# First pass of a fused attention and SwiGLU kernel: transposes and weight joins moved behind the masks, raw weights in six places

## The chip, the cores and the metric

The kernel runs on one core of one Trainium2 chip. The metric is device microseconds of one execution, the median of several runs. The engines are named as in the profile: PE (TensorE, with its weight loads PEld), DVE (VectorE), ACT (ScalarE), POOL (GpSimd), and SP, which here issues nearly all DMAs.

## The reference

```python
# q, k, v: (8, 8, 576, 64) float32; tau = 0.02
scores = q @ k.T / sqrt(64)
thresh = max(scores, axis=-1) - tau
scores = where(scores >= thresh, scores, -1e9)
attn = exp(scores - max(scores)) ; attn /= sum(attn) + 1e-9
x = (attn @ v) -> (B, H, S, D) to (B*S, H*D) = (4608, 512)
g = x @ w_gate                 # (512, 1536)
h = g * sigmoid(g) * (x @ w_val)
out = h @ w_out                # (1536, 512)
```

## The kernel before

The work is 32 pairs of heads (8 batches with 4 pairs each), and each pair has 576 queries and keys. A tile of attention is up to 128 queries of one pair. For one tile, PE computes the scores of both heads into PSUM (`scores`, L505), DVE takes the row maxima (L497), ACT makes a threshold (L528) and the exponentials (L529), and DVE masks them by the threshold and sums them (L532, then L534 and L535 for the reciprocal). After that PE transposes the masked scores (`flip_steps`, L576 or L578, L582 to L588), ACT copies the transposes to SBUF (L585, L592), and PE multiplies them with v (`attend_tile`, L609 and L611); ACT copies that result out (L614). The PSUM that holds a tile's scores is used again by the next tile, so the scores of the next tile wait for the masks of this one, head by head.

The first batch is done in two passes, in program order and in a schedule written out by hand. The first pass takes pairs 0 to 3 with two tiles of 128 queries each (n from 0 to 3, x from 0 to 1). The second takes the other three tiles of the same pairs (n from 4 to 7, in the order of pairs 3, 0, 1, 2), and between them PE does the first part of the feed-forward block (`fill`, L625). In one turn of the loop over tiles, program order is: scores and maxima of this tile; the point `maxima`; product with v of an earlier tile; exponentials of this tile; transposes of the tile before; the point `flipped`; masks of this tile; the point `masked`; scaled unit matrices (first pass, L548) or fill; the point `end`. At each point the table `STEPS` names side work that is put into the engines' queues there. Every engine works through its queue in order, so a step's place decides what it stands in front of. After the two passes the remaining batches run in an order that a planner (`Plan`) writes out.

The steps are these:

- `weights`, `weights 2`: `fetch_weights` issues on SP the two DMAs of one weight piece (or of two pieces) as raw 64-bit words (L344). A piece needs a free raw place, and a place comes free when its piece has been joined.
- `split`: ACT makes the upper part of a piece (L360). In the first pass POOL makes the lower part (L362) and clamps the upper one (L353). In the second pass ACT makes the lower part too (L364), and POOL clamps at `clamp_split`. The lower parts use three buffers by turns.
- `shift`: one DVE operation on the upper part (L383).
- `join`: one DVE operation that puts the sign back (L390) and, on POOL, the sum of both parts (L400), by `add_lower`.
- `qk`, `rest`: DMAs of a pair's k and first 256 columns of q, or of the rest of q (L436). `v`: DMAs of a pair's v (L479, L480).
- `scale`: POOL scales a q tile (L440), in the order pair 2, pair 3, rests of pairs 3, 0, 1, 2, pair 4.
- `prepare`: DVE transposes k and q of the next pair (L738, L742). `turn`, `turn last`: DVE transposes the rest of q of a pair (L797).

`STARTS` lists what SP issues ahead of the first tile, after the q and k of pairs 0 and 1.

Of the kernel before, what the change touches and what calls it, by code (L numbers as in the profile page):

```python
# [27 lines left out]
class Plan:  # L28
# [94 lines left out]

STARTS = ("weights", "v", "weights", "qk", "weights", "v", "v", "weights")

STEPS = {
    (0, 0, "flipped"): ("qk",),
    (0, 1, "maxima"): ("prepare",),  # L130
    (0, 1, "masked"): ("split",),
    (0, 1, "end"): ("scale",),
    (1, 0, "flipped"): ("split", "shift"),
    (1, 0, "masked"): ("join",),
    (1, 1, "flipped"): ("weights 2", "prepare"),
    (1, 1, "masked"): ("split", "shift"),
    (1, 1, "end"): ("join",),
    (2, 0, "maxima"): ("rest", "weights 2"),
    (2, 0, "flipped"): ("rest",),
    (2, 0, "masked"): ("shift", "scale", "split", "join"),  # L140
    (2, 0, "end"): ("weights 2",),
    (2, 1, "maxima"): ("scale", "prepare", "v", "rest"),
    (2, 1, "flipped"): ("rest", "split"),
    (3, 0, "flipped"): ("shift",),
    (3, 0, "end"): ("join",),
    (3, 1, "maxima"): ("shift", "split", "turn last"),
    (3, 1, "flipped"): ("weights 2", "scale", "prepare"),
    (3, 1, "masked"): ("split",),
    (3, 1, "end"): ("turn", "shift", "scale"),
    (4, 0, "flipped"): ("turn", "qk"),  # L150
    (4, 1, "maxima"): ("scale",),
    (4, 1, "masked"): ("scale",),
    (4, 2, "end"): ("turn",),
# [4 lines left out]
def kernel(  # L158
# [152 lines left out]
    wpieces = deque()  # L311
# [5 lines left out]
    for f in range(0, DFF, FW):  # L317
        for c in range(NCC):
            wpieces.append((wgv[:, :, c, f:f + FW], [w[c * P:(c + 1) * P, f:f + FW] for w in (w_gate, w_val)],
                            len(wpieces) % 4))  # L320
    nf = TW // DM2
    wplaces = deque([6, 4, 5, 3, 4, 5, 4, 5])
    for e in range(2):
# [5 lines left out]
    fetched, split, used = deque(), deque(), set()  # L329
    joined = []  # L330

    def fetch_weights(n=1):
        for _ in range(n):
            if not wpieces or wpieces[0][2] in used:
                return
            dst, srcs, place = wpieces.popleft()
            used.add(place)
            m = 2 if len(srcs) == 2 else nf
            to = places[place].bitcast(U64).rearrange("p (m n) -> p m n", m=m)
            if len(srcs) == 1:  # L340
                nc.sync.dma_start(out=to, in_=srcs[0])
            else:
                for x, src in enumerate(srcs):
                    nc.sync.dma_start(out=to[:, x, :], in_=src)  # L344
            fetched.append((dst, place))
# [30 lines left out]
    def shift_weights(n=1):  # L376

        steps = [split.popleft() for _ in range(min(n, len(split)))]
        if any(up is x for up, place, lo in steps for x in unclamped):
            clamp_split()  # L380
        for up, place, lo in steps:
            ub = up.bitcast(U32)
            nc.vector.tensor_scalar(out=ub, in0=ub, scalar1=3, scalar2=None, op0=ALU.logical_shift_left)  # L383
        shifted.extend(steps)

    def join_weights(n=None):
        steps = shifted[:n]
        for up, place, lo in steps:
            ub = up.bitcast(U32)
            nc.vector.scalar_tensor_tensor(out=ub, in0=words(place, up, 1), scalar=0x80000000, in1=ub,  # L390
                                           op0=ALU.bitwise_and, op1=ALU.bitwise_xor)
            used.discard(place)
        unsummed.extend(steps)
        del shifted[:n]
        add_lower(min(1, len(unsummed)))
# [311 lines left out]
    rest = list(range(TA, NT + 1))  # L707
# [19 lines left out]
    def prepare(seg):  # L727
        i = seg["i"]
        if i in kept:
            seg.update(kept[i])  # L730
            return
        assert i > NP or (i, 0) in scaled
        qr, kr = raws[i][0:2]
        if i < NP:
            kept[i] = None
            qT = qkp.tile([P, S], F32, name="qT")
            kT, rest_ = kTs[i], rests[i]
            nc.vector.transpose(out=kT, in_=kr)  # L738
            if i == 0:
                nc.vector.tensor_scalar(out=scl, in0=tau_s, scalar1=0.0, scalar2=SCALE, op0=ALU.is_ge, op1=ALU.mult)  # L740
                nc.vector.tensor_scalar(out=qr[:, 0:QA], in0=qr[:, 0:QA], scalar1=scl, scalar2=None, op0=ALU.mult)
            nc.vector.transpose(out=qT[:, 0:QA], in_=qr[:, 0:QA])  # L742
            if i == 0:
                nc.vector.tensor_scalar(out=cap, in0=tau_s, scalar1=0.0, scalar2=2e38, op0=ALU.is_ge, op1=ALU.mult)
                nc.vector.tensor_scalar(out=cap, in0=cap, scalar1=-1e38, scalar2=None, op0=ALU.add)
                nc.vector.scalar_tensor_tensor(out=cut, in0=tau_s, scalar=-1.0, in1=cap, op0=ALU.mult, op1=ALU.min)
            later.append((rest_, i))
            kept[i] = {"kT": kT, "qT": rest_, "q0": QA}
        else:
            qT, kT = qr, kr  # L750
            nc.vector.transpose(out=kT, in_=kT)
            nc.vector.transpose(out=qT, in_=qT)
        seg.update(kT=kT, qT=qT, q0=0)
# [25 lines left out]
    def start(what):  # L779
        if what == "weights":  # L780
            fetch_weights()
        elif what == "v":
            load_v(unloaded.popleft())
        elif what == "qk":
            fetch_qk(unfetched.popleft())
        else:
            rest_load()

    for what in STARTS:
        start(what)  # L790
    last = iter(())

    def turn():
        to, i = later.popleft()
        assert (i, 1) in scaled
        turned_rests.add(i)
        nc.vector.transpose(out=to, in_=raws[i][2])  # L797

    def steps(n, x, point):
        for what in STEPS.get((n, x, point), ()):  # L800
            if what in ("rest", "v", "qk"):
                start(what)
            elif what == "turn last":
                later.rotate(1)
                turn()
            elif what == "prepare":
                prepare(segs[n + 1])
            elif what == "weights 2":
                fetch_weights(2)
            else:  # L810
                {"scale": scale_next, "turn": turn, "split": split_weights, "shift": shift_weights,
                 "join": join_weights}[what]()

    begun = deque([scores(segs[0], 0, first_pss)])
    for n, seg in enumerate(segs[:2 * NP]):
# [3 lines left out]
        for x, t in enumerate(seg["tiles"]):  # L819
# [4 lines left out]
            if (n, x) == (0, 0):  # L824
                second_pss = [ps_s.tile([P, 2, 512], F32, name="sc") for _ in range(2)]
                begun.append(scores(seg, seg["tiles"][1], second_pss, later=True))
                next(begun[0])
            next(go)
            steps(n, x, "maxima")
            if n >= NP:  # L830
                join_weights(1)
# [51 lines left out]
            last = go  # L883
# [1673 lines left out]
    rest = [b for b in banks if b.fixed is None and b not in mine]  # L2557
# [213 lines left out]
```

## Time and profile before

| | |
|---|---|
| runs | 1331.33 us median of 3 (1331.12 to 1332.28) |
| the profiled execution | 1332.23 us, of which the span from first to last instruction is 1330.4 |
| granted TensorE clock | 1.000 |
| busy, share of the span | PE 99%, PEld 84%, DVE 82%, ACT 67%, POOL 71% |
| first pass, scores of (1,0) to scores of (4,0) | 15.24 to 46.29 us |
| second pass, up to the first scores of the planned part | 46.29 to 123.47 us |
| DMA | 209.81 MB, mean 158 GB/s |

Times of lines are in microseconds from the start of the span. The timeline merges instructions that follow each other on one engine and line; in brackets stands the idle time before, and what ended it. Busy times of PE are modelled ends. Nearly all of the span is the planned part, which starts where the second pass ends.

### The profile page before, as it was taken

The page shows a single profiled execution, that of the slowest core. Times are in us where ns is not written, and L with a number is a line of the kernel's source. Part 1 is how long each engine was busy: PE and PEld are TensorE (multiplying, and loading weights), DVE is VectorE, ACT ScalarE, POOL GpSimd, SP SyncE. Part 2 cuts the span into 40 slices and gives each one's busy share as a digit, 9 for nine tenths or more (in the row PEclk, how much of TensorE's full clock was granted, in tenths as well). Part 3 has the DMA queues.
Part 4 walks back from the last instruction along what each step waited for, and adds up shares of the span by engine and source line. Part 5 has one row for each costly group of instructions (what it writes and reads, how often), then busy time and mean ns, then how long its engine had stood idle before and what let it go on. Part 6 is the DMA issues. An engine that isn't in the chain of part 4 may idle for free.

```text
span 1330.4 us, 41756 instructions
## 1 busy us (share of the span) xinstructions
PE 1320.2 (99%) x16294; PEld 1119.1 (84%) x16294; DVE 1092.4 (82%) x2900; ACT 892.9 (67%) x2336; POOL 951.1 (71%) x1137
## 2 busy tenths in 40 slices
PE   8999999999999999999999999999999999999998
PEld 7777777777788878888888888887888889999998
DVE  7799988878887788878888887888788888767986
ACT  6898877677755777787777777777777775444300
POOL 3788597565695979756995779677975798866720
PEclk9999999999999999999999999999999999999999
DMA  8853334456647544656265746655465627465341
GB/s 178 220 180 108 71 81 120 126 155 178 161 168 228 168 152 114 202 157 222 71 203 165 235 107 193 180 166 154 111 202 157 217 74 227 152 208 189 96 171 40
DMA packets 230884, 209.81 MB, mean 158 GB/s; under 512 B 167968, under 2 KB 185376, under 8 KB 223008
## 3 DMA queue, kind: packets, MB, share of 16 engines
q1 hardware_dynamic: 226768, 206.22, 52.4%
q8 instruction: 129, 2.11, 0.7%
q10 hardware_dynamic: 3920, 0.92, 0.3%
q14 instruction: 67, 0.55, 0.1%
HBM read 169.08 MB, written 38.01 MB: 156 GB/s over the span
## 4 chain that ended last, share of the span: by engine, by line
PE 94%; ACT 3%; DMA 1%; POOL 1%; DVE 1%; SPq 1%; issue 0%; ACTq 0%; DVEq 0%
PE pb L1190 14%; PE px L1820 12%; PE sc L2111 10%; PE pa L1190 10%; PE xa L2211 10%; PE pe L1190 6%; PE po L1498 6%; PE sc L2601 5%; PE py L1820 4%; PE pe L1385 3%; PE pb L2601 2%; PE pg L1423 2%; PE pa L2601 2%; PE pv L1423 2%; PE py L1829 2%; PE sc L1820 1%
## 5 line engine op out<-in xcount | busy, mean ns | idle before, releaser
L2159 DVE SCALAR_TENSOR_TENSOR pall<-sc,th,pall 128x288 f32<-128x288 f32 x504 | 244.2, 514 | 39.3 <-ACT pall L2157 20.2
L2157 ACT ACTIVATE pall<-sc,nm 128x288 f32<-128x288 f32 x504 | 232.7, 497 | 34.9 <-DVE pall L2159 34.7
L1190 PE MATMUL pb<-xall,big 128*128 128x256 f32 x864 | 205.9, 381 | 0.0
L2189 DVE STREAM_TRANSPOSE pall<-pall 128x576 f32<-128x576 f32 x252 | 188.4, 764 | 19.2 <-ACT pall L2187 9.4
L971 POOL TENSOR_TENSOR big<-big 128x128 f32<-128x128 f32 (+3 forms) x226 | 167.1, 748 | 43.5 <-ACT big L1325 21.7
L2187 ACT ACTIVATE pall<-pall,ri 128x288 f32<-128x288 f32 x380 | 175.8, 527 | 27.3 <-DVE ri L2175 26.3
L1190 PEld LDWEIGHTS pb<-xall,big 128*128 128x128 f32 x864 | 161.0, 190 | 24.1 <-issue 2.2
L971 POOL TENSOR_TENSOR hall<-hall,tmp 128x512 f32<-128x512 f32 x80 | 102.1, 1278 | 87.9 <-DVE hall L1249 66.9
L2132 DVE TENSOR_REDUCE mx<-sc 128x2 f32<-128x576 f32 x168 | 125.5, 747 | 45.2 <-PE sc L2111 45.1
L2111 PE MATMUL sc<-kT,qT 64*32 64x288 f32 (+1 forms) x5376 | 144.5, 345 | 0.0
L1190 PE MATMUL pa<-xall,big 128*128 128x256 f32 x576 | 137.6, 382 | 0.0
L2111 PEld LDWEIGHTS sc<-kT,qT 64*32 64x32 f32 x5376 | 95.3, 106 | 48.3 <-issue 8.3
L2211 PE MATMUL xa<-pall,vall 64*32 64x288 f32 x4032 | 128.7, 404 | 0.0
L1190 PEld LDWEIGHTS pa<-xall,big 128*128 128x128 f32 x576 | 107.9, 190 | 17.3 <-issue 2.2
L2211 PEld LDWEIGHTS xa<-pall,vall 64*32 64x32 f32 x4032 | 74.0, 107 | 46.9 <-issue 4.0
L2184 POOL TENSOR_SCALAR pall<-pall,ri 128x288 f32<-128x288 f32 x124 | 63.5, 523 | 49.0 <-DVE ri L2175 46.9
L2168 ACT COPY sums<-sums 32x6 f32<-32x6 f32 x336 | 66.6, 198 | 31.3 <-DVE pall L2159 26.2
L1190 PE MATMUL pe<-xall,big 128*128 128x256 f32 x352 | 83.9, 381 | 0.0
L2134 DVE TENSOR_REDUCE mx<-sc 128x1 f32<-128x288 f32 x168 | 75.0, 447 | 0.0
L1190 PEld LDWEIGHTS pe<-xall,big 128*128 128x128 f32 x352 | 66.3, 190 | 10.3 <-ACT xlast L2223 0.7
L971 POOL TENSOR_TENSOR hall<-hall 128x384 f32<-128x384 f32 (+2 forms) x69 | 70.3, 1032 | 0.8
L971 POOL TENSOR_TENSOR big<-hall 128x384 f32<-128x384 f32 (+2 forms) x69 | 65.6, 972 | 4.3 <-PE pa L1190 4.2
(402 smaller groups left out, 3055.7 us busy)
## 6 DMA issues: line engine op xcount, KB each, us to landing
big<-sums_hbm SPq DMA_DIRECT2D x30, 1280.0 KB, 7.6
big<-sums_hbm SPq DMA_DIRECT2D x30, 1024.0 KB, 7.4
vall<-in_v_dram SPq DMA_DIRECT2D x112, 144.0 KB, 4.0
big<-sums_hbm SPq DMA_DIRECT2D x54, 256.0 KB, 3.6
sums_hbm<-big SPq DMA_DIRECT2D x36, 256.0 KB, 3.6
out_dram<-big SPq DMA_DIRECT2D x32, 256.0 KB, 3.1
qT<-in_q_dram SPq DMA_DIRECT2D x112, 72.0 KB, 4.2
kT<-in_k_dram SPq DMA_DIRECT2D x112, 72.0 KB, 3.0
```

The source lines that it names most:

```text
L971: nc.gpsimd.tensor_tensor(out=out, in0=a, in1=b, op=op)
L1190: nc.tensor.matmul(ps[:, i], w[:, k_, i * P:(i + 1) * P], x[:, k_, :], start=first and i == k_ == 0, stop=True, skip_group_check=True)
L1498: nc.tensor.matmul(ps, h(f), w[:, f, :], start=(f == 0), stop=(f == NF2 - 1))
L1820: nc.tensor.matmul(ps, a[:, f, :], ws[n][:, f, :], start=bank_ not in begun, stop=True, skip_group_check=True)
L2111: nc.tensor.matmul(pss[h][(slice(g * G, (g + 1) * G), *part)], qT[hs, col:col + G], kT[hs, c * SH + keys[0]:c * SH + keys[1]], start=True, ...
L2132: rs.append(job("DVE", 0.72, lambda n=n, tile_=tile_: nc.vector.tensor_reduce(out=mx[:, n:n + 2, 0], in_=tile_[:, :, 0:SH], axis=AX.X, op= ...
L2157: ej = job("ACT", 0.42, lambda x=x, n=n: nc.scalar.activation(ps[x], scs[x], AF.Exp, bias=nm[:, n:n + 1]), ej, masks.get((h, u - 1)), rank=0)
L2159: masks[x] = job("DVE", 0.45, lambda x=x, n=n: nc.vector.scalar_tensor_tensor(out=ps[x], in0=scs[x], scalar=th[:, n:n + 1], in1=ps[x], op0 ...
L2187: scaled.append(job("ACT", 0.46, lambda x=x, n=n: nc.scalar.activation(x, x, AF.Copy, scale=ri[:, n:n + 1]), rj, rank=rank))
L2189: seg["turned"].append(job("DVE", 0.72, lambda both=both: nc.vector.transpose(out=both, in_=both), *scaled, rank=rank))
L2211: nc.tensor.matmul(holds[a].ap()[x * G:(x + 1) * G, 0:SH].rearrange("d (i q) -> d i q", q=G), vr[rs, h, j, ds], p[rs, h, :, j, :], start=( ...
L2601: nc.tensor.matmul(both.ap(b_)[:, at_ * P:(at_ + 1) * P], ws[x], xd[x], start=b_ not in begun, stop=True, skip_group_check=True)
```

## The change

The table of steps of the first pass is written anew. `prepare` moves from the points in front of the masks to the point behind them, and joins move from the end of a tile to behind the masks of another one, so that a tile has either a `prepare` or a join there. The shift of (1,0) goes, and later shifts stand in the tile of their join. q and k of pair 3 are issued on SP among the `STARTS`, and not at (0,0). The first six raw weight pieces have a place each (the new ones lie in `xall` and `extra`), and later pieces go through the first four. The split at (2,0) goes; at the end of (4,0), in the second pass, a join, a fetch, a shift, a split and a clamp are added. `steps` knows `clamp` as a further step. The order of PE's instructions is the same in both kernels.

```diff
--- before.py
+++ after.py
@@ -123,31 +123,32 @@
 
 
 
-STARTS = ("weights", "v", "weights", "qk", "weights", "v", "v", "weights")
+STARTS = ("weights", "v", "weights", "qk", "weights", "v", "qk", "v", "weights")
 
 STEPS = {
-    (0, 0, "flipped"): ("qk",),
     (0, 1, "maxima"): ("prepare",),
     (0, 1, "masked"): ("split",),
     (0, 1, "end"): ("scale",),
-    (1, 0, "flipped"): ("split", "shift"),
-    (1, 0, "masked"): ("join",),
-    (1, 1, "flipped"): ("weights 2", "prepare"),
-    (1, 1, "masked"): ("split", "shift"),
-    (1, 1, "end"): ("join",),
-    (2, 0, "maxima"): ("rest", "weights 2"),
+    (1, 0, "flipped"): ("split",),
+    (1, 0, "masked"): ("prepare",),
+    (1, 1, "flipped"): ("shift",),
+    (1, 1, "masked"): ("split", "join",),
+    (1, 1, "end"): ("weights 2", "scale",),
+    (2, 0, "maxima"): ("rest",),
     (2, 0, "flipped"): ("rest",),
-    (2, 0, "masked"): ("shift", "scale", "split", "join"),
-    (2, 0, "end"): ("weights 2",),
-    (2, 1, "maxima"): ("scale", "prepare", "v", "rest"),
-    (2, 1, "flipped"): ("rest", "split"),
-    (3, 0, "flipped"): ("shift",),
-    (3, 0, "end"): ("join",),
-    (3, 1, "maxima"): ("shift", "split", "turn last"),
-    (3, 1, "flipped"): ("weights 2", "scale", "prepare"),
+    (2, 0, "masked"): ("prepare",),
+    (2, 1, "maxima"): ("scale", "v", "rest",),
+    (2, 1, "flipped"): ("rest", "split", "shift",),
+    (2, 1, "masked"): ("join",),
+    (2, 1, "end"): ("weights 2",),
+    (3, 0, "masked"): ("shift", "join",),
+    (3, 1, "maxima"): ("shift", "split", "turn last",),
+    (3, 1, "flipped"): ("weights 2", "scale", "prepare",),
     (3, 1, "masked"): ("split",),
-    (3, 1, "end"): ("turn", "shift", "scale"),
-    (4, 0, "flipped"): ("turn", "qk"),
+    (3, 1, "end"): ("turn", "shift", "scale",),
+    (4, 0, "flipped"): ("turn", "qk",),
+    (4, 0, "masked"): ("clamp",),
+    (4, 0, "end"): ("join", "weights 2", "shift", "split", "clamp",),
     (4, 1, "maxima"): ("scale",),
     (4, 1, "masked"): ("scale",),
     (4, 2, "end"): ("turn",),
@@ -317,7 +318,7 @@
     for f in range(0, DFF, FW):
         for c in range(NCC):
             wpieces.append((wgv[:, :, c, f:f + FW], [w[c * P:(c + 1) * P, f:f + FW] for w in (w_gate, w_val)],
-                            len(wpieces) % 4))
+                            len(wpieces) if len(wpieces) < 6 else (len(wpieces) - 6) % 4))
     nf = TW // DM2
     wplaces = deque([6, 4, 5, 3, 4, 5, 4, 5])
     for e in range(2):
@@ -809,7 +810,7 @@
                 fetch_weights(2)
             else:
                 {"scale": scale_next, "turn": turn, "split": split_weights, "shift": shift_weights,
-                 "join": join_weights}[what]()
+                 "join": join_weights, "clamp": clamp_split}[what]()
 
     begun = deque([scores(segs[0], 0, first_pss)])
     for n, seg in enumerate(segs[:2 * NP]):
```

## The prediction

> **What bounds the kernel now.** I read the busy table of the page, the windows over the stages, the chain of waits over the first 140 us, and then the timeline there, engine by engine. A tile is written (n,x) as in the code: n counts the pairs (0 to 3 first pass, 4 to 7 second), x the tiles of a pair.
>
> ```profile
> PE 1320.2 (99%) x16294; PEld 1119.1 (84%) x16294; DVE 1092.4 (82%) x2900; ACT 892.9 (67%) x2336; POOL 951.1 (71%) x1137
> 300.00:1310.00 1010.00, 1009.78 (x12867) 871.40 (x12866) 826.06 (x2228) 661.99 (x1766) 744.34 (x928) 1.00 0.55 166
> ```
>
> The first line is the page's, the second a window (PE busy is its second number). From 130 us on PE never waits; the change reorders only the first hundred rows of DVE, ACT, POOL and SP, and PE's order not at all. So a shift of the second pass reaches the end one for one, and only the first 70 us have to be worked out.
>
> In the first pass the chain is PE's, one scores block (L505) per tile:
>
> ```profile
> 20.71 1.25 PE L505 MATMUL sc<-pall,qT 64*128 64x288 f32 x8
> 25.48 1.73 PE L505 MATMUL sc<-pall,qT 64*128 64x288 f32 x8
> 30.74 1.61 PE L505 MATMUL sc<-pall,qT 64*128 64x288 f32 x8
> 36.04 1.94 PE L505 MATMUL sc<-pall,qT 64*128 64x288 f32 x8
> 51.92 1.57 PE L609 MATMUL xa<-big,vall 128*64 128x128 f32 x16 [0.31 <-ACT big L585]
> ```
>
> An undisturbed block takes 1.25 us and a tile 4.77 (20.71 to 25.48). Longer blocks wait for the second mask (L532) of the tile before, which frees the PSUM of the second head: the excess is the mask's end + 0.10 - the block's start in every row. At 51.92 PE waits for ACT's copies (L585), which stand behind the exponentials of (4,0). These are the rows behind that:
>
> ```profile
> 31.99 1.94 SPq L436 DMA_DIRECT2D hall<-in_q_dram  x4
> 38.80 0.85 POOL L440 TENSOR_SCALAR hall<-hall,scl 128x320 f32<-128x320 f32 x1 [2.06 <-DMA hall<-in_q_dram]
> 39.62 0.91 POOL L362 TENSOR_SCALAR big<-wo 128x768 f32<-128x768 uint32 x1
> 40.60 0.83 POOL L353 TENSOR_SCALAR big<-big 128x768 f32<-128x768 f32 x1
> 42.39 1.82 POOL L400 TENSOR_TENSOR big<-big,extra 128x768 uint32<-128x768 uint32 x1 [0.96 <-DVE big L390]
> 46.44 0.53 POOL L440 TENSOR_SCALAR hall<-hall,scl 128x320 f32<-128x320 f32 x1
> 47.01 0.51 DVE L797 STREAM_TRANSPOSE pall<-hall 128x320 f32<-128x320 f32 x1
> 47.45 0.82 DVE L383 TENSOR_SCALAR big<-big 128x768 uint32<-128x768 uint32 x1
> 48.19 1.41 DVE L497 TENSOR_REDUCE nm<-sc 128x1 f32<-128x576 f32 x2
> ```
>
> POOL scales pair 3's rest of q (38.80) as soon as its load, issued at 31.99, has landed. Pair 0's rest is scaled at 46.44; DVE turns it (L797) the moment that is done, and the maxima of (4,0) come behind that turn.
>
> **Turning and joins behind the masks.** In (1,1), (2,0), (2,1), (3,0) the 1.02 us of `prepare` (L738 0.69, L742 0.33) and the 0.87 of a join (L390) leave the stretch between maxima and masks, or the place in front of the next maxima. Undisturbed, a block at s has its maxima at s+1.27 and its second mask ends 3.38 later, at s+4.65; with the 0.10 that is s+4.75 against 4.77 for the tile: it just fits. A shift in front of the masks is free (maxima +1.34, shift 0.48, mask at +1.82, where the second exponential holds the second mask anyway). Behind the masks, `prepare` ends at s+6.0 and the next maxima begin at s+4.77+1.27 = s+6.04: also fits. Blocks then start at 20.71, 25.48, 30.25, 35.02, 39.79 and (4,0) at 44.56, not 46.29: -1.73. In (3,0) shift and join together (1.35) hold up the maxima of (3,1) by 0.3, so (4,0) waits 0.66 instead of 0.36. Alone this is -1.4 us.
>
> **The SP queue.** Pair 3's q and k (8 issues) now go ahead of v of pair 2 (4) and weight piece 3 (2), and pieces 4 and 5, which have places of their own, are issued one behind the other ahead of pair 3's rest. That rest had one piece ahead of it after pair 3's q; now it has pieces 3, 4, 5. Before: piece 4 issued at 31.12, last of the rest landed about 38.75, 7.6 later. After: from 20.73, 12 issues at 0.60 to 0.64 and one slow one (+0.75) put piece 3 at 29.1. A piece is 768 KB written, 2.1 us at the 365 GB/s of the window 34 to 35. So T, the landing, is 29.1 + 7.6 + 2 x 2.1 = 40.9 (bounds: 36.4, if the rest issued by 34.3 lands in the 2.1 us of pair 3's q; 42, if the issues wait longer for the eight before them). I take 40.9: the DMA engines are full from 33 to 38 in the trace, and four q loads issued there took 5.3 us.
>
> The Trainium skill (DMA: Bandwidth & Descriptors, Anatomy of one DMA) puts a DMA at about 2.0 us fixed plus bytes over 436 GB/s, fitted on another issue path. By it, an estimate, the rest lands near 36.8, the first rival. The trace disagrees for these loads of 128-byte runs: 5.3 us for 40 KB.
>
> **POOL.** Its order changes: the scaling of pair 3's rest (L440) now stands directly behind that of pair 3's q (before, a lower part, a clamp and a sum stood between), and POOL waits there from 30 to T. Queued behind it: lower part and clamp of piece 3 (L362 0.97, L353 0.92), two sums that were ready long ago (L400, 2 x 1.87), lower part and clamp of piece 4 (0.96, 0.9), and only then the scaling of pair 0's rest (0.53). With 0.65 for the first scaling that is 8.7 us by start-to-start rows with DVE beside it, 8.3 without; I take 8.6. DVE's turn, at its own pace due at 45.6, waits until 49.6, against 47.01 before: 2.6 to 2.7 late. The maxima of (4,0) follow at about 50.9 instead of 48.19, and the masks, which no PE block waits for within 3 us. But ACT's exponentials stand ahead of its copies of (3,1): PE's xa block starts 3.06 after the maxima (0.79 to the threshold, 1.01 to the second exponential, 0.62 to the copy, 0.64 to PE), at 53.9 instead of 51.92. The -1.4 is gone, and +2.0 stands.
>
> **One step less, made up for.** A split (ACT L360) leaves (2,0), where ACT is not late: 0. It returns at the end of (4,0) with its lower part on ACT (L360 0.82 + L364 0.92 = 1.74), where ACT idles 1.89 before its copy at 58.48: 0 by itself. But L364 writes a buffer that the sum of piece 4 reads, and POOL reaches that sum late: rescaling L540 4.72 after the maxima (1.65), clamp 0.9, sum 1.85. L364 waits 0.7, of which 0.15 is slack: +0.5. POOL's additional clamp and sum (0.85 + 1.87) exceed its idle 2.4 around 58 to 62, and the clamp that the chain goes through at 67.76 comes another 0.2 late. DVE's additional shift and join (1.5) lie in 3.64 idle us ahead of 57.71: 0.
>
> **Sum.** +2.0 + 0.5 + 0.2 = +2.7 us. The profiled execution took 1332.23 (span 1330.40 and 1.83 around it), 0.9 over the median of 1331.33; it becomes 1334.9, the median 1334.0. A measurement of this kernel can tell about 0.2%, 2.66 us, from no change: the forecast lies on that line.
>
> **Rivals.**
> - The rest lands by 37.5. POOL then reaches pair 0's scaling by 46, DVE hardly waits, and -1.4 with +0.3 for L364 gives 1330.2. For it: the DMA engines idle at 30 to 32 us (share 0.34 and 0.39) and might take loads earlier. Against it: two more pieces ahead. It decides below T = 38; faster by over 0.2% would need 2.66 us, and the whole excess of the scores blocks from (2,0) on is about 2.1.
> - Landing at 38 to 39.5: gain and wait cancel, 1331.3.
> - POOL's backlog does not clear at 67 us: each of six more L364 of the second pass waits about 0.5 for a sum, +5 to +6 in all, 1337. For it: POOL is 8 to 10 us busy in each 10 us there; against it: POOL waits 1.4 for ACT at 70.12. It decides if T passes 42.
> - The change does nothing visible, its waits hidden by the copies: 1331.3.
>
> **Chances.** Forecast 0.62, of which 0.38 above the line and 0.24 below it, since what the rows leave unpriced (contention on POOL, semaphores) adds rather than takes; early landing 0.12 (0.03 beyond the line); cancelling 0.10; backlog 0.14; nothing 0.02. Slower 0.38 + 0.14 = 0.52, same 0.24 + 0.09 + 0.10 + 0.02 = 0.45, faster 0.03. T between 39.5 and 42, with 0.3 either way for POOL's 8.6, makes the forecast 1332.3 to 1335.4; the range also takes the cancelling case and most of the backlog, and leaves out most of the early landing: 1330.4 to 1337.0.
>
> **What would show it.** The timeline after should have scores blocks of 1.25 us from (2,0) to (3,1), starting near 25.5, 30.3, 35.0, 39.8; POOL idle some 10 us before a scaling of `hall` near 41, put down to a DMA; DVE idle 3 to 4 us before L797 near 49.6, put down to POOL L440; L364 waiting for L400 near 60. If POOL's scaling starts before 38, the SP step is wrong; if it starts at 41 and the xa block is not late, the ACT step is.

## The result: 3.7 us slower, and the profile after

| | before | after |
|---|---|---|
| median | 1332.38 us (8 runs) | 1336.12 us (8 runs) |
| the profiled execution, and its span | 1332.23, 1330.4 | 1335.99, 1334.2 |
| granted TensorE clock | 1.000 | 0.997 |
| first scores of the planned part | 123.47 | 127.17 |

The ratio is 1.0028, 95% interval 1.0019 to 1.0037, so +2.5 to +4.9 us. The planned part starts 3.70 us later and the span is 3.8 us longer: all of the loss lies in the two passes of the first batch. Behind them the two kernels differ by 0.1 us.

PE's timeline after shows where. Each row is start, duration, engine, line, operation and tile; every line number is one higher than before (scores are L506, the product with v L610).

```profile
20.46 1.25 PE L506 MATMUL sc<-pall,qT 64*128 64x288 f32 x8
25.23 1.77 PE L506 MATMUL sc<-pall,qT 64*128 64x288 f32 x8
30.53 1.25 PE L506 MATMUL sc<-pall,qT 64*128 64x288 f32 x8
35.31 1.25 PE L506 MATMUL sc<-pall,qT 64*128 64x288 f32 x8
40.09 1.25 PE L506 MATMUL sc<-pall,qT 64*128 64x288 f32 x8
46.37 3.11 PE L506 MATMUL sc<-pall 64*128 64x288 f32 x10 [1.43 <-DVE pall L533]
...
55.07 0.38 PE L610 MATMUL xa<-big,vall 128*64 128x128 f32 x2
...
59.63 1.36 PE L506 MATMUL sc<-pall 64*128 64x288 f32 x10
64.64 1.19 PE L514 MATMUL sc<-pall 64*64 64x288 f32 x8 [0.35 <-DVE pall L533]
...
127.17 1.72 PE L2112 MATMUL sc<-kT,qT 64*32 64x288 f32 x64
```

Up to (3,1) the blocks are nearly what the change promises: 1.25 us in (2,1), (3,0) and (3,1), where before had 1.61, 1.94 and 1.25. Then PE waits 1.43 us for the masks of (3,1), the block of (4,0) takes 3.11 us instead of 1.72, and the product with v stands at 55.07 where it stood at 51.92. POOL's timeline shows what lies behind it:

```profile
39.69 0.53 POOL L441 TENSOR_SCALAR hall<-hall,scl 128x320 f32<-128x320 f32 x1 [9.75 <-DMA hall<-in_q_dram]
40.19 0.91 POOL L363 TENSOR_SCALAR extra<-wo 128x768 f32<-128x768 uint32 x1
41.18 1.01 POOL L354 TENSOR_SCALAR big<-big 128x768 f32<-128x768 f32 x1
42.16 4.60 POOL L401 TENSOR_TENSOR big<-big 128x768 uint32<-128x768 uint32 x2
46.84 0.89 POOL L363 TENSOR_SCALAR big<-xall 128x768 f32<-128x768 uint32 x1
47.81 0.83 POOL L354 TENSOR_SCALAR big<-big 128x768 f32<-128x768 f32 x1
48.74 0.53 POOL L441 TENSOR_SCALAR hall<-hall,scl 128x320 f32<-128x320 f32 x1
```

POOL stands still for 9.75 us in front of the scaling of pair 3's rest, then works off a queue of six instructions before it scales pair 0's rest at 48.74 (46.44 before). Two sums take 4.60 us, where two took 2 x 1.82 before. DVE runs beside them:

```profile
40.28 1.23 DVE L384 TENSOR_SCALAR big<-big 128x768 uint32<-128x768 uint32 x1
41.54 1.46 DVE L391 SCALAR_TENSOR_TENSOR big<-wo,big 128x768 uint32<-128x768 uint32 x1
42.92 1.41 DVE L498 TENSOR_REDUCE nm<-sc 128x1 f32<-128x576 f32 x2
44.25 0.83 DVE L384 TENSOR_SCALAR big<-big 128x768 uint32<-128x768 uint32 x1
...
49.30 0.51 DVE L798 STREAM_TRANSPOSE pall<-hall 128x320 f32<-128x320 f32 x1 [1.95 <-POOL hall L441]
...
59.18 2.17 DVE L384 TENSOR_SCALAR big<-big 128x768 uint32<-128x768 uint32 x1 [1.22 <-POOL big L354]
61.27 1.41 DVE L498 TENSOR_REDUCE nm<-sc 128x1 f32<-128x576 f32 x2
```

A shift (L384) takes 0.55 us alone and 0.80 to 2.17 beside POOL's operations in these tiles, a join (L391) 0.94 and up to 1.46; the maxima (L498) take 1.41 or 1.42 for two, whatever POOL does. The last two rows are (4,1): a shift of 2.17 us stands directly in front of its maxima.

The windows give PE's share of each microsecond second in the row, and the granted clock third from the end:

```profile
45.00:46.00 1.00, 0.00 (x0) 0.00 (x0) 1.00 (x3) 1.00 (x4) 1.00 (x1) 1.00 0.52 84
47.00:48.00 1.00, 1.00 (x7) 0.96 (x6) 0.32 (x2) 1.00 (x3) 0.92 (x2) 0.61 0.63 177
53.00:54.00 1.00, 1.00 (x6) 1.00 (x6) 0.89 (x2) 1.00 (x4) 1.00 (x1) 0.50 1.01 295
54.00:55.00 1.00, 1.00 (x12) 0.88 (x11) 0.96 (x5) 0.55 (x3) 0.63 (x1) 0.97 0.58 157
```

PE does nothing from 45 to 46, and from 47.2 to 54.1 it runs at half clock. Before, the clock is 1.00 in all of these windows.

### The profile page after: what moved, and what is told of

Its sections match the earlier page's. It is cut to its first block, busy times and chain, and to the rows that moved or that the text cites. A ratio compares the mean times of both kernels' runs of the same rounds, so it can differ in the third digit from the quotient of the medians.

```text
span 1334.2 us, 41749 instructions
## 1 busy us (share of the span) xinstructions
PE 1322.5 (99%) x16294; PEld 1122.0 (84%) x16294; DVE 1096.3 (82%) x2900; ACT 894.2 (67%) x2337; POOL 951.8 (71%) x1136
## 4 chain that ended last, share of the span: by engine, by line
PE 92%; ACT 2%; SPq 2%; DMA 1%; DVE 1%; POOL 1%; issue 1%; ACTq 0%; DVEq 0%; POOLq 0%
PE pb L1191 14%; PE px L1821 12%; PE sc L2112 10%; PE pa L1191 10%; PE xa L2212 9%; PE pe L1191 6%; PE po L1499 6%; PE sc L2602 5%; PE py L1821 4%; PE pe L1386 3%; PE pb L2602 2%; PE pg L1424 2%; PE pa L2602 2%; PE pv L1424 2%; PE py L1830 2%; PE sc L1821 1%
## 5 line engine op out<-in xcount | busy, mean ns | idle before, releaser
L2133 DVE TENSOR_REDUCE mx<-sc 128x2 f32<-128x576 f32 x168 | 125.5, 747 | 45.6 <-PE sc L2112 45.2
```

The source lines that it names most:

```text
L2133: rs.append(job("DVE", 0.72, lambda n=n, tile_=tile_: nc.vector.tensor_reduce(out=mx[:, n:n + 2, 0], in_=tile_[:, :, 0:SH], axis=AX.X, op= ...
```

## The experiments

Theory: POOL's order costs the time. The scaling of pair 3's rest blocks the head of POOL's queue until its DMA lands, and what piles up behind it delays first DVE's shifts, then DVE's turn of pair 0, then ACT's copies. Rival 1: the DMA itself is the limit, wherever the scaling stands. Rival 2: PE's half clock is the loss. A second question is the end of (4,0), where the prediction put a wait of L364.

Loads before the first tile differ by up to 1 us between executions, so the table counts every start from the scores of (1,0). Times of whole runs resolve about 0.1%, 1.2 us; smaller differences are read from the traces, one for each kernel. Five kernels (scale_late, late_no_clamp, four_los, short_shift and short_shift_four) have the same steps in the same order up to (4,0), and yet their scores of (4,0) start between 30.14 and 30.63: what differs by less than 0.5 us between two rows of a column is not resolved. The distance of the scores of (4,2) from those of (4,1) repeats better: it is 5.08 to 5.15 in scale_late, rest_first, both and four_los.

| kernel | scores (4,0) | product with v in (4,0) | scores (4,1) | scores (4,2) | planned part | median, ratio to before (interval) |
|---|---|---|---|---|---|---|
| before | 31.05 | 36.68 | 41.20 | 45.79 | 108.23 | |
| after | 31.38 | 40.08 | 44.64 | 49.65 | 112.18 | 1336.12, 1.0028 (1.0019 to 1.0037) |
| scale_late | 30.14 | 36.11 | 40.62 | 45.73 | 108.24 | 1333.06, 0.9999 (0.9990 to 1.0009) |
| rest_first | 30.78 | 36.75 | 41.27 | 46.35 | 108.88 | 1332.94, 0.9998 (0.9989 to 1.0008) |
| both | 30.27 | 36.24 | 40.76 | 45.91 | 108.44 | 1332.81, 0.9999 (0.9990 to 1.0009) |
| pe_busy | 31.82 | 38.77 | 44.97 | 49.89 | 112.20 | 1336.64, 1.0026 (1.0016 to 1.0035) |
| two_fillers | 31.77 | 38.73 | 43.24 | 49.04 | 111.52 | 1336.37, 1.0030 (1.0019 to 1.0040) |
| late_no_clamp | 30.47 | 36.44 | 40.96 | 47.67 | 111.67 | 1334.83, 1.0015 (1.0006 to 1.0024) |
| best | 30.81 | 36.83 | 41.35 | 48.76 | 112.69 | 1336.74, 1.0031 (1.0019 to 1.0042) |
| four_los | 30.63 | 36.60 | 41.12 | 46.23 | 109.43 | 1332.94, 1.0005 (0.9996 to 1.0014) |
| short_shift | 30.40 | 36.37 | 40.89 | 45.68 | 108.26 | 1332.48, 0.9998 (0.9989 to 1.0008) |
| short_shift_four | 30.57 | 36.55 | 41.06 | 45.84 | 107.76 | 1332.50, one run |

All edits are against after, unless another kernel is named.

### scale_late: the scaling later in POOL's queue

```diff
-    (2, 1, "maxima"): ("scale", "v", "rest",),
+    (2, 1, "maxima"): ("v", "rest",),
-    (3, 0, "masked"): ("shift", "join",),
+    (3, 0, "masked"): ("scale", "shift", "join",),
```

> The scaling of pair 3's rest moves from (2,1) to (3,0), ahead of that tile's shift and join; only POOL's order changes. Theory A (POOL stands 9.8 us before that scaling, and its two sums then run beside DVE's shifts and joins of (3,0) and (3,1)): one sum is done before the rest lands, L441 of hall still starts near 39.7 but with no more than 2 us of idle before it, the scores of (4,0) start at 45.0 to 45.5 instead of 46.37, no half clock, planned part at 123 to 124 instead of 127.17, time 1332 to 1333. Theory B (DVE's own shift and join between the masks of (3,0) and (3,1) set the scores of (4,0)): they start at 46.2 or later, time 1335.5 to 1336.5.

The loss is gone: the planned part starts 3.94 us earlier than in after, counted from (1,0). POOL's timeline:

```profile
37.07 1.83 POOL L401 TENSOR_TENSOR big<-big 128x768 uint32<-128x768 uint32 x1
39.66 0.53 POOL L441 TENSOR_SCALAR hall<-hall,scl 128x320 f32<-128x320 f32 x1 [0.75 <-DMA hall<-in_q_dram]
...
45.67 0.53 POOL L441 TENSOR_SCALAR hall<-hall,scl 128x320 f32<-128x320 f32 x1
```

The DMA lands when it did (39.66 against 39.69); only what stands in front of the waiting instruction is different. The idle time falls from 9.75 to 0.75 us, and pair 0 is scaled 3.07 us earlier. Rival 1 falls. Since the half clock goes too, this run does not yet part theory and rival 2.

PE's timeline of this kernel is also the first with the change's gain in it:

```profile
45.19 2.06 PE L506 MATMUL sc<-pall 64*128 64x288 f32 x10 [0.72 <-DVE pall L533]
...
55.67 1.36 PE L506 MATMUL sc<-pall 64*128 64x288 f32 x10
60.78 1.19 PE L514 MATMUL sc<-pall 64*64 64x288 f32 x8 [0.45 <-DVE pall L533]
```

The scores of (4,0) come 0.91 us earlier than before and those of (4,1) 0.58. But those of (4,2) follow (4,1) by 5.11 us, against 4.59 before, and the gain is spent.

Not all of the 3.94 us is POOL's order. By the scores of (3,1) this execution is already 0.53 us ahead of after, because its block of (2,0) takes 1.25 us and not 1.77: a weight piece landed later here, POOL's lower part starts at 23.39, behind DVE's shift of (1,1) (23.13, 0.55 us), and in after at 22.86, ahead of it (23.07, 1.11 us). The four other kernels with these steps up to (4,0) have the slower block, 1.63 to 1.66 us; their scores of (4,0) are 0.42 to 0.65 us earlier than before and those of (4,1) 0.08 to 0.31. Their product with v starts at 36.37 to 36.60, against 40.08 in after: the loss is gone in all five.

### rest_first: pair 3's rest issued ahead of two weight pieces

```diff
-    (1, 1, "end"): ("weights 2", "scale",),
+    (1, 1, "end"): ("scale",),
-    (2, 0, "flipped"): ("rest",),
+    (2, 0, "flipped"): ("rest", "weights 2",),
```

> Weight pieces 4 and 5 are issued behind the rests of pairs 3 and 0 instead of ahead of them; only SP's order changes. Theory A (the two pieces ahead cost the rest about 2.1 us each of DMA time): the scaling of pair 3's rest starts near 35.5 instead of 39.69, POOL's sums are done before DVE needs it, planned part at 123 to 124, time 1332 to 1333. Theory B (the rest's landing is set by the latency of its small packets, not by what is ahead): the scaling starts at 38.5 or later, time 1335.5 to 1336.5.

```profile
36.76 0.53 POOL L441 TENSOR_SCALAR hall<-hall,scl 128x320 f32<-128x320 f32 x1 [6.83 <-DMA hall<-in_q_dram]
```

POOL's scaling starts at 36.76 after an idle time of 6.83 us, between the two expectations, 2.93 us earlier than in after, and 3.3 of the 3.95 us come back with POOL's order untouched. So either of the two, the order or the landing, gives back most of the loss. 6.83 us of idle POOL cost little here; they cost once the backlog behind them lies beside DVE's shifts and in front of DVE's turn of pair 0.

### both

The two edits together.

> The late scaling and the early rest together. Theory A (one wait, removed twice): no better than the better of the two by more than 0.5 us, 1331.5 to 1332.5. Theory B (POOL's place and SP's order are two costs that add): 1 us or more below the better of the two.

108.44, no better than scale_late alone: it is one wait, removed twice.

### pe_busy: PE kept busy in its idle time at (4,0)

```diff
+            if (n, x) == (NP, 0):
+                idle = bank("idle")
+                for _ in range(4):
+                    nc.tensor.matmul(idle[:, 0:224], ones[:, 0:P], ones[:, 0:224], start=True, stop=True)
+                give_back(idle)
```

The four matmuls of constants stand ahead of the scores of (4,0).

> Four matmuls on constants (about 1.8 us) are put ahead of the scores of (4,0), into a free PSUM bank, where PE stood idle for 1.4 to 1.9 us; nothing else changes. Theory A (PE's idle time brings the clock to 0.50 from 47 to 54 us, and that costs 1.5 to 2 us): no half clock there, planned part at 125.2 to 125.7, time 1334 to 1334.6. Theory B (the half clock has another cause, or is hidden by waits on DVE): planned part at 127 or later, time 1336 to 1336.5.

The half clock of 47 to 54 us is gone, and the time is not better. PE now waits where the prediction said it would, for ACT's copies:

```profile
53.99 1.57 PE L610 MATMUL xa<-big,vall 128*64 128x128 f32 x16 [1.55 <-ACT big L586]
```

Behind this second idle time the clock halves again, from 55.6 to 59.0 (0.50 in the window 56 to 57). The product with v comes 2.09 us later than before (38.77 against 36.68): this is POOL's and DVE's lateness alone, without the clock (the maxima of (4,0) wait for DVE's turn and shift here too, not for the delayed scores).

### two_fillers: both idle times filled

pe_busy with three more matmuls of constants ahead of the product with v in (4,0).

> The kernel pe_busy (4 matmuls of constants ahead of the scores of (4,0)) with 3 more matmuls of constants ahead of the product with v at (4,0), where PE idled 1.55 us in pe_busy. They add to the work of PE in its two long idle times and take nothing away. Theory A: the granted clock falls to 0.50 after an idle of 1.5 us and the half clock costs time of its own: without both idles it stays at 1.00 from 40 to 70 us, PE's blocks from (4,0) to (4,2) take full-speed times, and the planned part starts earlier than 127.2 (after 127.17, pe_busy 127.42), by up to the 1.7 us that half clock added to PE's blocks, less what POOL's sum for L365 takes back: 125.8 to 126.8, time 1334.8 to 1336.0. Theory B: the half clock only fills time in which PE would wait for ACT anyway, so nothing moves: 127.2 to 127.5, 1336.3 to 1336.7.

```profile
54.74 1.57 PE L610 MATMUL xa<-big,vall 128*64 128x128 f32 x16 [0.22 <-ACT big L586]
```

The clock stays at 1.00 from 44 to 66 us. The planned part starts 0.66 us earlier than in after, which the times don't resolve (1336.37 is the time of theory B); 3.29 of the 3.95 us remain. Rival 2 falls as the main cause: the half clock makes the product with v 1.35 us later (40.08 against 38.73), but half of that is lost again behind it: the scores of (4,2) follow those of (4,1) by 5.80 us instead of 5.01, since the shift ahead of the maxima of (4,1), which stands behind POOL's clamp and sum, ends only 0.60 us earlier (61.77 against 61.35, or 45.76 against 46.36 from (1,0)).

The runs without a trace say the same by their mean granted clock over the span, which 6.84 us at half clock bring down to 0.997. Of the eight runs of after, three are at 0.997 and took 1335.97 to 1337.33 us; the one at 1.000 took 1337.35, the longest of the eight. Of the ten runs of pe_busy eight are at 1.000, and they took 1335.07 to 1337.38. So the loss is there without that half clock too.

### late_no_clamp: is it POOL's clamp that delays the second pass?

scale_late without one step (`shift` then issues the clamp itself, since it needs a clamped piece):

```diff
-    (4, 0, "masked"): ("clamp",),
```

> The kernel after with scale_late's edit (the scaling of pair 3's rest is named at (3,0), masked), and without the clamp at (4,0), masked. Theory A: what scale_late won in the first pass (0.6 us by the scores of (4,1), counted from the scores of (1,0)) went back because POOL's clamp L354 of (4,0) waits for ACT's split in front of the sum of piece 4 (L401), for which ACT's L365 waits 0.45 us at 57. Without the clamp there the sum stands in front: L365 waits for nothing, the scores of (4,2) follow those of (4,1) by 4.6 instead of 5.11, the planned part starts 0.4 to 0.5 earlier than in scale_late (122.8 against 123.29), and the time is 0.4 to 0.5 below scale_late's, 0.1 us either side of that of the kernel before. Theory B: the sum is late because POOL has too much to do, whatever the order: L365 waits as before, 5.1 between the scores, time as scale_late (ratio to before 1.000).

ACT's L364 (L365 in after) no longer waits, as theory A said, and yet the time is 1.8 us worse than scale_late's. (In this kernel and in best lines have the numbers of before.) DVE's timeline says why:

```profile
57.49 2.16 DVE L383 TENSOR_SCALAR big<-big 128x768 uint32<-128x768 uint32 x1 [2.63 <-POOL big L353]
59.58 1.41 DVE L497 TENSOR_REDUCE nm<-sc 128x1 f32<-128x576 f32 x2
```

The shift at the end of (4,0) waits 2.63 us for the clamp, which now stands behind the sum, and the maxima of (4,1) stand behind the shift. PE waits 2.06 us for the masks, and the clock halves again. ACT's wait was not what set the time; the theory had looked at the wrong queue.

### best: five steps placed by hand

```diff
-    (1, 0, "flipped"): ("split",),
+    (1, 0, "flipped"): ("split", "shift"),
-    (1, 1, "flipped"): ("shift",),
-    (2, 1, "maxima"): ("scale", "v", "rest",),
+    (2, 1, "maxima"): ("v", "rest",),
-    (3, 0, "masked"): ("shift", "join",),
-    (3, 1, "maxima"): ("shift", "split", "turn last",),
+    (3, 0, "flipped"): ("shift",),
+    (3, 0, "masked"): ("scale", "join",),
+    (3, 1, "maxima"): ("split", "turn last",),
-    (3, 1, "end"): ("turn", "shift", "scale",),
+    (3, 1, "end"): ("turn", "shift", "shift", "scale",),
-    (4, 0, "masked"): ("clamp",),
```

> The kernel after with five steps moved: the scaling of pair 3's rest is named at (3,0), masked; no clamp at (4,0), masked; the shift of (1,1) back at (1,0), flipped; the shift of (3,0) in front of its masks (flipped) and not behind them; the second shift of (3,1) from the maxima to the end. Prepare and joins stay behind the masks. Theory A (the idea of the change is sound, its gain of about 1.7 us was lost to POOL's order and to shifts beside sums): scores blocks of 1.25 us at a distance of 4.77 to the end of the first pass, scores of (4,0) at 44.5 to 45 against 46.29 before, no wait of L365, planned part at 121.9 to 122.6 against 123.47, time 1331.0 to 1331.8 where the kernel before takes 1332.6 (ratio 0.9988 to 0.9994). Theory B (the second pass has its own limit, POOL's and DVE's backlog, and takes any gain of the first pass back): planned part 123.2 to 123.6 and the time of the kernel before.

```profile
37.65 1.84 DVE L383 TENSOR_SCALAR big<-big 128x768 uint32<-128x768 uint32 x1
```

Theory A was wrong in both of its parts, and the planned part, at 127.73, is far from theory B's too. Without the clamp of (4,0) it has late_no_clamp's wait of 2.63 us, and the shift of (3,0), moved in front of the masks, took 1.84 us beside a POOL sum (37.27 to 39.08), so that PE waited 0.49 at (3,1). A shift in front of the masks is not free when POOL sums beside it.

### four_los: a fourth buffer for lower parts, so that ACT needn't wait

scale_late with:

```diff
+    fourth_lo = xall[:, XW:XW + TW]
-    los = deque([extra[:, 4 * S + 2 * TW:], rall[:, 4 * S:], obs[:, 0:TW]])
+    los = deque([extra[:, 4 * S + 2 * TW:], rall[:, 4 * S:], obs[:, 0:TW], fourth_lo])
...
+        los.remove(fourth_lo)
```

> scale_late with a fourth buffer for lower parts in the first two passes (dead space of xall; dropped again before the planned part), so that L365 at the end of (4,0) writes a buffer that no unfinished sum reads. No step moves. Theory A: of the 0.5 us that the scores of (4,2) come late in scale_late (5.11 after those of (4,1), 4.59 before), L365's wait of 0.45 carries the path through ACT's copy and threshold (58.49), and the shift in front of the maxima, which takes 2.17 beside POOL's sums, carries the path through the maxima (threshold possible at 58.19). Without the wait the threshold is bound by the maxima: 0.3 of the 0.5 comes back, scores 4.8 apart, planned part 0.3 earlier than in scale_late counted from the scores of (1,0) (107.9 against 108.24), time 1332.7 or so, which can't be told from 1333.06. Theory B: L365's wait is covered by ACT's idle time behind it, and the shift alone sets the path: scores 5.1 apart, 108.2. Theory C: the buffer lets POOL's clamp and sums and DVE's shift change places further on and the whole 0.5 comes back: 4.6 apart, 107.7.

```profile
56.97 1.02 ACT L366 ACTIVATE big<-wo,minus 128x768 f32<-128x768 uint32 x1
61.16 1.19 PE L515 MATMUL sc<-pall 64*64 64x288 f32 x8 [0.45 <-DVE pall L534]
```

ACT's lower part (L366 here) runs at 56.97 without a wait, where it waited 0.45 us in scale_late. The threshold comes 0.28 us earlier after the scores of (4,1), but the masks stand behind DVE's shift, maxima and join and do not, and the scores of (4,2) still follow those of (4,1) by 5.11 us: theory B. The end of the second pass is 0.7 us longer than in scale_late, with a wait of 1.96 us of ACT for a DMA to `xall`, where the fourth buffer lies; no step of the change is in that.

### short_shift and short_shift_four: the shift of (4,0) taken away

scale_late and four_los, in which the shift at the end of (4,0) covers 1 of 768 columns; the rest of this shift is left out of the computation.

```diff
+            ub = ub if columns is None else ub[:, 0:1, 0:columns]
             nc.vector.tensor_scalar(out=ub, in0=ub, scalar1=3, scalar2=None, op0=ALU.logical_shift_left)
...
-    (4, 0, "end"): ("join", "weights 2", "shift", "split", "clamp",),
+    (4, 0, "end"): ("join", "weights 2", "short shift", "split", "clamp",),
```

> scale_late, but DVE's shift at the end of (4,0), the one that stands in front of the maxima of (4,1), covers 1 of 768 columns of its piece; the rest of that shift is left out. Theory A (DVE's queue sets the second pass: the shift of 2.17 us, blocked beside POOL's sum, holds up the maxima by 0.46, and all behind them): the maxima of (4,1) begin 1.27 us after the scores, and of the 0.52 us by which the scores of (4,2) come late (5.11 against 4.59) 0.2 to 0.5 comes back; the smaller figure if ACT's L365, which waits 0.45 as before, then holds the threshold. Theory B (L365's wait alone sets it): 5.1 as in scale_late.

> four_los with the same shortened shift: neither L365's wait nor the shift is left in front of the threshold. Theory A: scores of (4,2) 4.6 to 4.75 us after those of (4,1), as in the kernel before (4.59), where four_los has 5.11 with the whole shift. Theory B (something else of the second pass, such as the join beside POOL's sum, holds the masks): over 5.0.

DVE's timeline of short_shift:

```profile
55.73 0.15 DVE L388 TENSOR_SCALAR big<-big 128x1 uint32<-128x1 uint32 x1 [0.72 <-POOL big L354]
57.35 1.42 DVE L502 TENSOR_REDUCE nm<-sc 128x1 f32<-128x576 f32 x2 [1.47 <-PE sc L510]
58.69 1.40 DVE L395 SCALAR_TENSOR_TENSOR big<-wo,big 128x768 uint32<-128x768 uint32 x1
60.00 0.80 DVE L537 SCALAR_TENSOR_TENSOR pall<-sc,th,pall 128x576 f32<-128x576 f32 x1
```

The maxima now wait for PE, 1.27 us after the scores at 56.08, as before. The scores of (4,2) follow by 4.79 us, with or without ACT's wait (4.79 and 4.78). So the shift carries 0.32 of the 0.52 us that the second pass loses, and ACT's wait none of it. Most of the other 0.2 us fits the join behind the maxima, which takes 1.40 us beside POOL's sum and 0.95 in the kernel before; that was read from the rows and not tried by itself.

## Why the prediction was right or wrong

Predicted was +2.7 us, a median of 1334.0; measured +3.7, 1336.12. Another 1.05 us of the difference is the kernel before, whose median in the same runs was 1332.38 and not 1331.33. The direction and the chain from POOL's wait through DVE's turn to ACT's copies were right. Three steps were not, and part of the agreement in size was luck.

- **Turning and joins behind the masks.** Right: the blocks of (2,1) to (3,1) are 1.25 us at a distance of 4.78. Too good by a little: (2,0) still takes 1.77, since the shift of (1,1), ahead of the masks there, took 1.11 us at 23.07 beside a lower part of POOL (22.86 to 23.77). A shift in front of the masks was called free. So the scores of (3,1) come 1.18 us earlier (25.10 against 26.28 from (1,0)) rather than the 1.73 that the equal distances gave.
- **The SP queue.** Landing at 39.69, predicted 40.9, inside its bounds. SP issued piece 3 0.75 us earlier than worked out. The earlier landing that the prediction weighed against it, 36.8, did not come.
- **POOL.** Right in mechanism: from the landing to the end of pair 0's scaling 9.6 us, predicted 8.6; the errors of the two steps nearly cancel, and DVE's turn is at 49.30, predicted 49.6. The 1.0 us more is the sums, 4.68 from start to start instead of 2 x 1.87: the first took 2.51 us and the second 2.13, beside DVE's join and shift. (They were not both "ready long ago" either, since the join of the second ended at 43.0, but the first was still running then.) Without the half clock the product with v is 2.05 us later than before (two_fillers), predicted +2.0. That these two meet is luck: the landing came 1.2 us earlier and the queue took 1.0 longer than predicted.
- **The first failed step: "DVE's turn, at its own pace due at 45.6".** It took DVE's rows as they are beside an idle POOL. A lower part, a clamp and a sum that POOL's wait had held up (the sum runs at 37.07 in scale_late, at 42.16 here) now lay beside the shifts and the join of (3,0) and (3,1), and these took 1.23, 1.46 and 0.83 us (0.79, 0.96 and 1.06 in scale_late). So DVE's masks of (3,1) were late, PE waited 1.43 us for them, and the gain of 1.4 at (4,0) became a loss of 0.33. Of the 1.24 us between this and scale_late's gain of 0.91, 0.71 arise behind the scores of (3,1), and 0.53 are the shift of (1,1). The gain itself was put too high: without the backlog it is 0.42 to 0.91 us in five traces. By their rows, the shift of (1,1) lies beside a lower part in four of them (0.97 to 1.00 us), and in scale_late the shift of (3,1) beside a sum (1.06 us). DVE for its part waited only 1.95 us for the turn, not 3 to 4: it was late itself. The Trainium skill (SBUF — State Buffer, Who interferes with whom) says that DVE and GpSimd share a pair of ports under an exclusive lock: a DVE operation in a two-port mode, which a `tensor_scalar` can enter, and a GpSimd operation block each other for a whole instruction, one with two SBUF inputs contends with a GpSimd operation that reads SBUF, and a `tensor_reduce` never contends on trn2. The rows shown agree: the shift of 2.18 us in four_los ends 0.42 us behind the sum that it started beside (57.89 against 57.47), and the maxima take 1.41 or 1.42 throughout.
- **The second: PE at full clock.** Not in the sum at all. In the profiled execution it made the product with v 1.35 us later than POOL's lateness alone, of which 0.66 reaches the planned part (two_fillers); not every run has it.
- **The third: the end of (4,0).** The size was near, +0.42 in after (5.01 against 4.59) for +0.5, the mechanism was not. L364 (L365 after) waits 0.36 us for the sum, where 0.7 was predicted, but in scale_late's order, where it waits 0.45, taking this wait away changes nothing (four_los). What costs is the shift that the prediction set at 0, because shift and join "lie in 3.64 idle us" of the kernel before (`57.71 1.42 DVE L497 TENSOR_REDUCE nm<-sc 128x1 f32<-128x576 f32 x2 [3.64 <-PE sc L505]`). Those idle us existed, but the shift has to wait for POOL's clamp, which waits for ACT's split, and then for the sum that POOL starts first. It ended at 61.35 in after; the maxima were due at 60.90, 1.27 us behind their scores.
- **The additional clamp and sum, +0.2:** from the scores of (4,2) to the planned part it is 62.53 us after and 62.44 before, 0.1.

The rival of an early landing was tested by rest_first: with the landing at 36.76 the planned part starts 0.65 us later than before and not 1.1 earlier, as that rival said: only 0.27 us is won at (4,0), where PE still waits 0.96 for the masks, and the second pass takes more than that. The test is not a clean one: weight piece 3 lands later there, ACT waits 0.53 us for it at 35.95, and the block of (3,1) takes 1.65 us. The backlog rival did not come: behind (4,2) nothing more is lost.

So, from (1,0), the lateness is 0.33 us at the scores of (4,0), 3.40 at the product with v (2.05 without the half clock), 3.44 at the scores of (4,1), 3.86 at those of (4,2) and 3.95 at the planned part. No version here that does the whole computation beats the kernel before by more than the runs resolve. With POOL's order mended the change gains 0.08 to 0.58 us up to (4,1) in five traces, and pays 0.52 for the steps that moved into the second pass.

## What to carry to other kernels

When a step moves to a place where its DMA has not landed, list everything behind it in that engine's queue, and cost those instructions at the time at which they will then run, with what will run beside them. Free time on an engine is usable only from the moment at which the step's inputs are ready; an idle stretch that ends in front of critical work hides nothing for an instruction that becomes ready at its end. A wait named in the profile is only a suspect: here one wait was removed (four_los) without any effect on the next scores, since another queue, DVE's, ended later.

## What the runs showed of the hardware that was not expected

- PE's granted clock fell to 0.50 after idle times of 1.43 (after), 1.55 (pe_busy), 2.06 (late_no_clamp) and 2.75 us (best). Worked out from the windows, where a mean of 0.61 is a share of 0.78 at half clock, it stayed there for 6.84, 3.40, 3.42 and 3.42 us. It did not fall after 0.72 (scale_late), 0.96 (rest_first) and 1.06 us (best). Length alone does not decide it: an idle time of 1.58 us in the first tiles (ahead of 12.60 in before) left the clock at 1.00, and the mean clock of the same kernel differs between runs (0.997 to 1.000 in after). The Trainium skill (TensorE: Matmul & The Clock Gate, What's actually happening) has the clock halve after at least one idle window of about 3.4 us that runs free of the kernel. The steps of 3.4 us fit such a window; an idle time of 1.43 us was enough here, and the measurement decides.
- One shift of 128x768 words on DVE takes 0.55 us alone and up to 2.18 beside POOL's sums. Whichever starts first runs undisturbed in these rows: in four_los POOL's sum runs from 55.64 to 57.47, the shift from 55.71 to 57.89, and the next sum, from 57.42, takes 2.13 us instead of 1.82; in scale_late the shift of (1,1), ahead of a lower part by 0.26 us, takes 0.55, and the lower part 1.04 instead of 0.91. Not every row fits: in after a shift that starts at 56.07, inside POOL's rescaling (L541, 55.47 to 57.15), takes 0.56 us.
